# Up products of a second MoE: a bilinear algorithm of 20 products in place of Strassen's 7, its output blocks gathered from five accumulating chains

## Chip, cores, metric

One core of one Trainium2 chip. The metric is the device time of one launch in microseconds (us), less is better. The engines are TensorE (PE: matmuls; PEld: its weight loads), VectorE (DVE), ScalarE (ACT), GpSimd (POOL) and SyncE (SP, which issues the DMAs).

## The reference, cut to what matters

A clustered attention and a first MoE make x of 1536 tokens by 512 features. The change lies in what follows, the second MoE, and in how its operands are prepared:

```python
def _moe2_ref(x, w_gate, w1, w2):        # x 1536x512, 8 experts, w1[e] 512x1024, w2[e] 1024x512
    logits = x @ w_gate
    logits = logits - logits.max()
    P = np.exp(logits)
    for _ in range(8):                   # Sinkhorn: the gate
        P /= P.sum(1, keepdims=True) + 1e-09
        P /= P.sum(0, keepdims=True) + 1e-09
        P *= N / E
    out = np.zeros((N, D), dtype=np.float32)
    for e in range(E):
        h = np.maximum(x @ w1[e], 0.0)   # the "up" products
        ye = h @ w2[e]                   # the "down" products
        out += P[:, e:e + 1] * ye
    return out
```

## The kernel before

Every fp32 operand of a matmul is held as two fp32r parts, a high one (rounded by ScalarE) and a low one (what is left, by a subtraction on GpSimd or VectorE). A product of two operands is three matmuls into one PSUM bank, high by low, low by high, high by high: `three`, lines 826 to 830, so nearly all matmuls of the profile stand at L828, L829 and L830.

x (the first MoE's output, `x2[0..3]`, one tile for each 128 features, tokens along the free dimension) stays in SBUF. The second MoE runs through 32 units, `seq`: 8 experts by 4 pairs of 128 hidden features. A unit n takes 512 features by 256 hidden features of w1 and 256 by 512 of w2, each brought by one DMA of 512 KB (`fetch_w`, line 963, on the SyncE queue, two buffers in all). `up_weights` (line 970) and `down_weights` (line 991) make the high parts on ScalarE and the low parts on GpSimd one unit ahead. `w_tile` hands out weight tiles from a ring of 10.

Up products. The tokens are cut in halves (rows 1 and 2 of a 2x2 block matrix, 768 tokens each) and the features in halves (columns). Units 1 to 31 use Strassen's algorithm in Winograd's form, `up_products` (line 1180): 7 products of block sums, with the sums of x (`s1` to `s4`) made once by `sum_blocks` (line 1043: additions on VectorE, splits on ScalarE and GpSimd), half of them while the first MoE ends and half in unit 0; the sums of the weights (`t1` to `t4`) are made for every unit. Each half of 768 tokens is done in two passes, 512 columns and then 256:

```python
    HALF = N // 2
    PASSES = [(0, TM), (TM, HALF - TM)]
    WAYS = {(0, 0): "uuuu", (0, 1): "uudddudddudd", 0: "uuduuduudud", 1: "uuddudududududd"}
```

Unit 0 runs without the algorithm (`up_blocks`, line 1171), as the sums aren't ready. A product sums over two blocks of 128 features, so it is 2 x 3 matmuls, 7 x 2 x 3 a pass. The results combine on VectorE (L1188 to L1205), `relu` (line 1166) makes the high part of h on ScalarE and the low part on VectorE (L1169). PSUM has four banks for the up products (`bank`, line 835, used in turn) and four for the down products (`pools["l2"]`).

Down products. `down` (line 1209): one step ("d") is one block of 128 tokens, 6 matmuls of 512 columns, and one VectorE operation that adds the result times the gate's weight to the accumulator (L1236; L1231 while the expert is the first). The steps of a pass are done during the next pass. `WAYS` (line 1246) writes out the order of up (u) and down (d) steps on TensorE by hand; the loop of lines 1247 to 1280 follows it and puts the weights' preparation, the DMAs and the gate's pieces between them. Nothing of the second MoE goes through the planner that orders the attention.

The gate. `gates` (line 1103) adds the last logits, transposes them and runs the eight Sinkhorn iterations, one piece at each `next(gate)` in units 0 to 3: a small matmul (L1141) and eight small VectorE operations (L1133 to L1148). Its PSUM tiles come from `bank`.

Of the kernel before, what the change touches and what calls it, by code (L numbers as in the profile page):

```python
# [151 lines left out]
def moe_kernel(ctx: ExitStack, tc: tile.TileContext, qk, nat, cen, wt, w123, wout, wgate, w1, w2, out):  # L152
# [681 lines left out]

    def bank(shape, name):

        l1_pools.append(l1_pools.pop(0))
        return l1_pools[0].tile(shape, F32, tag="l1", name=name)
# [118 lines left out]
    HALF = N // 2  # L957
    PASSES = [(0, TM), (TM, HALF - TM)]
# [10 lines left out]

    def up_weights(n):  # L970

        if n >= len(seq):
            return
        raw = raws.pop((0, n))
        src = {"b11": raw[:, 0, : 2 * P], "b21": raw[:, 0, 2 * P :], "b12": raw[:, 1, : 2 * P], "b22": raw[:, 1, 2 * P :]}
        use = ("b11", "b21", "b12", "b22")
        if n > 0:
            use = ("b11", "t2", "b21", "t3", "t1", "t4", "b22")
            ts = m_p.tile([P, 2 * MC], I32, tag="ta", name=f"ts{n}").bitcast(F32)
            ts = ts.rearrange("p (t d) -> p t d", t=4)  # L980
            src.update((f"t{k + 1}", ts[:, k]) for k in range(4))
            for t, a, b in (("t1", "b12", "b11"), ("t2", "b22", "t1"), ("t3", "b22", "b12"), ("t4", "t2", "b21")):
                nc.gpsimd.tensor_sub(src[t], src[a], src[b])
            yield
        for key in use:
            w = wop[n, key] = w_tile(f"wop{n}_{key}").rearrange("p (l d) -> p l d", l=2)
            nc.scalar.copy(w[:, 0], src[key])  # L987
            nc.gpsimd.tensor_sub(w[:, 1], src[key], f32(w[:, 0]))  # L988
            yield
# [28 lines left out]
    s_p = [ctx.enter_context(tc.tile_pool(name="s_p0", bufs=1, reuse_waits="tile"))]  # L1018
# [7 lines left out]
    def tmp(name, n):  # L1026
        return tmp_p.tile([P, TM], F32, tag="tmp", bufs=6, name=name)[:, :n]


    half = lambda d, h, o, n: [x2[d][:, l, h * HALF + o : h * HALF + o + n] for l in range(2)]  # L1030
    sums = {}

    def operand(key, k, o, n):

        if key in ("a11", "a12", "a21", "a22"):
            return half(2 * (int(key[2]) - 1) + k, int(key[1]) - 1, o, n)
        if key == "s1":
            return half(k, 1, o, n)
        return [sums[key, k][:, l, o : o + n] for l in range(2)]

    s1_tile = {}

    def sum_blocks(k, i, late):

        o, n = PASSES[i]
        if i == 0:
            for key in ("s2", "s3", "s4"):
                sums[key, k] = s_p[k].tile([P, 2, HALF], F32R, tag=key, name=f"{key}_{k}")
            if late is not None:
                s1_tile[k] = tmp_p.tile([P, HALF], F32, tag="s1", name=f"s1_{k}")  # L1050
        v = {}

        def made(key, fn, *args):
            v[key] = tmp(f"{key}_{o}_{k}", n) if late is None or key != "s1" else s1_tile[k][:, o : o + n]
            fn(v[key], *args)

        def split(key):
            hi, lo = operand(key, k, o, n)
            nc.scalar.copy(hi, v[key])
            nc.gpsimd.tensor_sub(lo, v[key], f32(hi))  # L1060

        for key in ("a21", "a22", "a11", "a12"):
            made(key, nc.vector.tensor_add, *map(f32, operand(key, k, o, n)))
            yield
        made("s1", nc.vector.tensor_add, v["a21"], v["a22"])
        yield
        made("s3", nc.vector.tensor_sub, v["a11"], v["a21"])
        yield
        made("s2", nc.vector.tensor_sub, v["s1"], v["a11"])
        yield  # L1070
        made("s4", nc.vector.tensor_sub, v["a12"], v["s2"])
        yield
        for key in ("s2", "s3", "s4"):
            split(key)
            yield
        if late is None:
            split("s1")
        else:
            late.append(lambda: split("s1"))

    kept = []
    first = up_weights(0)
    blocks = iter(())
    for n, _ in enumerate(mixed):
        if n == M_LAST - drain + 1:
            blocks = iter(g for i in range(2) for g in sum_blocks(0, i, kept))
        for _ in range(2):
            next(blocks, None)
        if n >= M_LAST - drain + 2 and n % 4 == 0:
            next(first, None)  # L1090
    for _ in (*first, *blocks):
        pass
# [4 lines left out]
    s_p.append(ctx.enter_context(tc.tile_pool(name="s_p1", bufs=1, reuse_waits="tile")))  # L1097
# [3 lines left out]


    def gates():
# [6 lines left out]
        tt = bank([P, NT, 2, E], "tt")  # L1110
# [9 lines left out]
        tp = bank([P, P], "gtp")  # L1120
# [4 lines left out]
        bc = bank([P, 1], "gbc")  # L1125
# [5 lines left out]
        for it in range(SINKHORN):  # L1131
# [7 lines left out]
            cs = bank([P, NT, E], f"cs{it}")  # L1139
# [12 lines left out]
    def product(ps, n, key, xkey, o, c, first):  # L1152
        for k in range(2):
            w = wop[n, key][:, :, k * P : (k + 1) * P]
            hi, lo = operand(xkey, k, o, c)
            three(ps, w[:, 0], w[:, 1], hi, lo, first and k == 0, k == 1, not first)

    hs = {}

    def h_tile(n, i, key, c):  # L1160

        h = h_p.tile([P, c // (2 * P), 2, 2 * P], F32R, tag=f"h{i}", bufs=4, name=f"h{n}_{i}_{key}")
        hs[n, i, key] = h
        return h

    def relu(h, z):
        z = z.rearrange("p (s t) -> p s t", t=2 * P)
        nc.scalar.activation(h[:, :, 0], z, AF.Relu)  # L1168
        nc.vector.scalar_tensor_tensor(h[:, :, 1], z, 0.0, f32(h[:, :, 0]), op0=ALU.max, op1=ALU.subtract)  # L1169

    def up_blocks(n, i):
        o, c = PASSES[i]
        for key in ("21", "22", "11", "12"):
            ps = bank([P, TM], f"z{n}_{i}_{key}")[:, :c]
            product(ps, n, f"b1{key[1]}", f"a{key[0]}1", o, c, True)
            product(ps, n, f"b2{key[1]}", f"a{key[0]}2", o, c, False)
            relu(h_tile(n, i, key, c), ps)
            yield

    def up_products(n, i):  # L1180
        o, c = PASSES[i]
        x, y, z, w = (bank([P, TM], f"{t}{n}_{i}")[:, :c] for t in "xyzw")
        a, u2, u3, c22, c21, c12 = (tmp(f"{t}{n}_{i}", c) for t in ("a", "u2_", "u3_", "c22_", "c21_", "c12_"))
        product(x, n, "b11", "a11", o, c, True)
        nc.scalar.copy(a, x)
        yield
        product(y, n, "t2", "s2", o, c, True)
        nc.vector.tensor_add(u2, y, a)  # L1188
        yield
        product(x, n, "b21", "a12", o, c, False)  # L1190
        relu(h_tile(n, i, "11", c), x)
        yield
        product(y, n, "t3", "s3", o, c, False)
        nc.vector.tensor_add(u3, y, a)
        yield
        product(z, n, "t1", "s1", o, c, True)
        nc.vector.tensor_add(c22, z, u3)  # L1197
        relu(h_tile(n, i, "22", c), c22)
        yield
        product(w, n, "t4", "a22", o, c, True)  # L1200
        nc.vector.tensor_sub(c21, u3, w)
        relu(h_tile(n, i, "21", c), c21)
        yield
        product(z, n, "b22", "s4", o, c, False)
        nc.vector.tensor_add(c12, z, u2)  # L1205
        relu(h_tile(n, i, "12", c), c12)
        yield

    def down(n, i):
        e, p = seq[n]  # L1210
        o, c = PASSES[i]
        for r in (1, 0):
            for t in range(c // P):
                ts = slice(t % 2 * P, (t % 2 + 1) * P)
                tt = (r * HALF + o) // P + t
                last = n == len(seq) - 1

                pieces = 2 if last and i == 1 and r == 0 and t == c // P - 1 else 1
                for piece in range(pieces):
                    cs = slice(piece * DM // pieces, (piece + 1) * DM // pieces)  # L1220
                    l2 = pools["l2"].tile([P, DM], F32, tag="l2", name=f"l2_{n}_{r}_{o}_{t}_{piece}")[:, cs]
                    for j in range(2):
                        h, w = hs[n, i, f"{r + 1}{j + 1}"], wdn[n, j]
                        h = h[:, t // 2, :, ts]
                        three(l2, h[:, 0], h[:, 1], w[:, 0, cs], w[:, 1, cs], j == 0, j == 1)
                    a = acc[tt][:, cs]
                    if n == 0:
                        nc.scalar.copy(a, l2)
                    elif e == 0:

                        nc.vector.tensor_add(a, l2, a)  # L1231
                        if p == PAIRS - 1:
                            assert next(gate, None) is None
                            nc.vector.tensor_scalar(a, a, prob[:, tt, :1], None, op0=ALU.mult)
# [95 lines left out]
```

## Time and profile before

| | |
|---|---|
| three runs | 1450.41, 1451.54, 1452.12 us (median 1451.54) |
| profiled execution, span from first to last instruction | 1448.8 us |
| the second MoE in it, first up matmul to the end | 446.1 to 1448.8 us |
| busy in the span | TensorE 99%, VectorE 63%, GpSimd 42%, ScalarE 35% |

The span is the profiled execution's own time as its page gives it; a run's time is that and what lies before the first and behind the last instruction. A matmul's duration in a row overlaps that of the next one, as matmuls are pipelined: the distance between two starts is what one costs. In the same way two VectorE operations that follow each other without a wait start closer together than the first one's duration.

### The profile page before, as it was taken

The page shows a single profiled execution, that of the slowest core. Times are in us where ns is not written, and L with a number is a line of the kernel's source. Part 1 is how long each engine was busy: PE and PEld are TensorE (multiplying, and loading weights), DVE is VectorE, ACT ScalarE, POOL GpSimd, SP SyncE. Part 2 cuts the span into 40 slices and gives each one's busy share as a digit, 9 for nine tenths or more (in the row PEclk, how much of TensorE's full clock was granted, in tenths as well). Part 3 has the DMA queues.
Part 4 walks back from the last instruction along what each step waited for, and adds up shares of the span by engine and source line. Part 5 has one row for each costly group of instructions (what it writes and reads, how often), then busy time and mean ns, then how long its engine had stood idle before and what let it go on. Part 6 is the DMA issues. An engine that isn't in the chain of part 4 may idle for free.

```text
span 1448.8 us, 20593 instructions
## 1 busy us (share of the span) xinstructions
PE 1430.4 (99%) x7900; PEld 1199.8 (83%) x7900; DVE 912.0 (63%) x1627; ACT 510.8 (35%) x1115; POOL 602.2 (42%) x691
## 2 busy tenths in 40 slices
PE   6999999999999999999999999999999999999999
PEld 5778787888878888888888888888888888888887
DVE  6888885355448577665655565655565655665655
ACT  6778776122124422222222222222222222222221
POOL 7666641565637433233333233333233343333320
PEclk9999999999999999999999999999999999999999
DMA  8665621112120110000110000110000110000102
GB/s 247 175 162 153 161 57 40 47 58 74 51 67 30 44 45 30 29 30 29 45 44 30 30 29 30 44 44 30 29 30 30 45 44 30 30 30 30 44 15 87
DMA packets 32210, 83.26 MB, mean 57 GB/s; under 512 B 4688, under 2 KB 10224, under 8 KB 32112
## 3 DMA queue, kind: packets, MB, share of 16 engines
q1 hardware_dynamic: 32112, 81.95, 19.0%
q8 instruction: 62, 1.02, 0.3%
q14 instruction: 36, 0.29, 0.1%
HBM read 65.46 MB, written 3.19 MB: 47 GB/s over the span
## 4 chain that ended last, share of the span: by engine, by line
PE 96%; DMA 1%; POOL 1%; DVE 1%; ACT 0%; issue 0%; SPq 0%; POOLq 0%; DVEq 0%
PE l L828 12%; PE l L829 12%; PE l L830 12%; PE y L605 4%; PE t L591 4%; PE z L830 3%; PE z L829 3%; PE z L828 3%; PE m L828 3%; PE m L830 3%; PE m L829 3%; PE y L830 3%; PE x L830 3%; PE y L829 3%; PE x L829 3%; PE y L828 3%
## 5 line engine op out<-in xcount | busy, mean ns | idle before, releaser
L1236 DVE SCALAR_TENSOR_TENSOR acc<-l,prob,acc 128x512 f32<-128x512 f32 (+1 forms) x337 | 251.7, 747 | 126.1 <-PE l L830 122.7
L828 PE MATMUL l<-w,h 128*128 128x512 f32 (+1 forms) x770 | 302.5, 393 | 0.0
L829 PE MATMUL l<-w,h 128*128 128x512 f32 (+1 forms) x770 | 301.5, 392 | 0.0
L830 PE MATMUL l<-w,h 128*128 128x512 f32 (+1 forms) x770 | 299.2, 389 | 0.0
L1168 ACT ACTIVATE h<-c 128x512 fp32r<-128x512 f32 (+1 forms) x186 | 97.6, 525 | 368.6 <-DVE c L1197 190.7
L988 POOL TENSOR_TENSOR wop_t<-ts,wop_t 128x256 fp32r<-128x256 f32 x124 | 91.3, 746 | 244.2 <-ACT wop_t L987 244.2
L988 POOL TENSOR_TENSOR wop_b<-wraw,wop_b 128x256 fp32r<-128x256 f32 x97 | 79.3, 818 | 258.5 <-ACT wop_b L987 258.5
L1169 DVE SCALAR_TENSOR_TENSOR h<-c,h 128x512 fp32r<-128x512 f32 (+1 forms) x186 | 112.6, 605 | 110.0 <-ACT h L1168 110.0
L830 PEld LDWEIGHTS l<-w,h 128*128 128x128 f32 x770 | 144.6, 188 | 31.5
L828 PEld LDWEIGHTS l<-w,h 128*128 128x128 f32 x770 | 145.4, 189 | 24.4
L829 PEld LDWEIGHTS l<-w,h 128*128 128x128 f32 x770 | 145.4, 189 | 22.6
L998 POOL TENSOR_TENSOR w<-wraw,w 128x512 fp32r<-128x512 f32 x64 | 82.9, 1296 | 96.7 <-ACT w L997 96.7
L569 DVE TENSOR_SCALAR_CACHE_REDUCE e<-s 128x768 f32<-128x768 f32 x96 | 90.9, 951 | 19.2 <-PE s L558 12.0
L1168 ACT ACTIVATE h<-x 128x512 fp32r<-128x512 f32 (+1 forms) x62 | 30.4, 491 | 186.7 <-PE x L830 186.7
L577 ACT ACTIVATE e<-e,nm 128x768 f32<-128x768 f32 x96 | 89.7, 935 | 4.3 <-DVE e L569 4.0
L828 PE MATMUL m<-x,mhi 128*128 128x512 f32 x216 | 84.7, 392 | 0.4 <-POOL x L260 0.4
L591 PE MATMUL t<-ident,e 128*128 128x128 f32 x576 | 81.1, 277 | 3.4 <-ACT at L253 3.0
L830 PE MATMUL m<-x,mhi 128*128 128x512 f32 x216 | 84.1, 389 | 0.0
L829 PE MATMUL m<-x,mlo 128*128 128x512 f32 x216 | 84.1, 389 | 0.0
L830 PE MATMUL x<-x,wop_b 128*128 128x512 f32 (+1 forms) x248 | 83.3, 336 | 0.0
L830 PE MATMUL y<-s,wop_t 128*128 128x512 f32 (+1 forms) x248 | 83.3, 336 | 0.0
L829 PE MATMUL y<-s,wop_t 128*128 128x512 f32 (+1 forms) x248 | 83.3, 336 | 0.0
(201 smaller groups left out, 3025.9 us busy)
## 6 DMA issues: line engine op xcount, KB each, us to landing
wraw<-in_w SPq DMA_DIRECT2D x64, 512.0 KB, 4.0
mraw<-in_w SPq DMA_DIRECT2D x18, 512.0 KB, 3.6
raw<-in_qk SPq DMA_DIRECT2D x16, 384.0 KB, 4.0
nat<-in_nat SPq DMA_DIRECT2D x15, 384.0 KB, 4.3
v<-in_nat SPq DMA_DIRECT2D x16, 192.0 KB, 3.0
r<-row SPq DMA_DIRECT2D x16, 192.0 KB, 3.3
mraw<-in_wout SPq DMA_DIRECT2D x8, 384.0 KB, 3.0
opsb<-opm SPq DMA_DIRECT2D x15, 192.0 KB, 2.6
```

The costliest lines, as they stand in the source:

```text
L569: lambda e: nc.vector.tensor_scalar(ex(), scores(), -SCALE, None, op0=ALU.mult, op1=ALU.min, accum_out=nm()),
L577: lambda e: nc.scalar.activation(ex(), ex(), AF.Exp, bias=nm(), scale=-1.0, accum_out=sm()[:, n]),
L591: nc.tensor.transpose(t()[:, c, ks], ex()[:, c, ks], ident)
L605: nc.tensor.matmul(y()[c * D : (c + 1) * D], v()[:, c * (NQ // 2) + k], at()[:, :, c, k * P : (k + 1) * P], start=k == 0, stop=k == NQ // ...
L828: nc.tensor.matmul(ps, whi, xlo, start=first, stop=False, skip_group_check=more)
L829: nc.tensor.matmul(ps, wlo, xhi, start=False, stop=False, skip_group_check=more)
L830: nc.tensor.matmul(ps, whi, xhi, start=False, stop=last, skip_group_check=more)
L988: nc.gpsimd.tensor_sub(w[:, 1], src[key], f32(w[:, 0]))
L998: nc.gpsimd.tensor_sub(w[:, 1], raw[:, j], f32(w[:, 0]))
L1168: nc.scalar.activation(h[:, :, 0], z, AF.Relu)
L1169: nc.vector.scalar_tensor_tensor(h[:, :, 1], z, 0.0, f32(h[:, :, 0]), op0=ALU.max, op1=ALU.subtract)
L1236: nc.vector.scalar_tensor_tensor(a, l2, prob[:, tt, e : e + 1], a, op0=ALU.mult, op1=ALU.add)
```

## The change

The tokens are cut into three blocks of 512 (t = 0, 1, 2), the features into four of 128 (k), the hidden features of a unit into two of 128 (j). A 3x4 by 4x2 block product has 24 products of 128 by 128 by 512; the new algorithm has 20, each of one combination of x blocks (some are x's own blocks) and one combination of weight blocks. There is one pass of 512 columns, and each product is one `three`. The products are grouped in five chains; a chain is one PSUM bank into which its products add up, and what a bank holds after some of them is read by VectorE or ScalarE into the six output blocks, in SBUF, with a sign. Chain m has ten products, nine of them followed by a read on VectorE and one (10) by a read on ScalarE. Chains a, b, c and d share two banks, chain m takes two in turn, and the gate moves to the down products' banks. Unit 0 does the 24 products without the algorithm (`direct`).

```diff
+    SUMS = ("c20", "tmp", "c00", "c11", "c21", "c01", "c10")
+    cell = lambda t, k: [x2[k][:, l, t * TM : (t + 1) * TM] for l in range(2)]
...
+    CHAINS = {"a": (0, 17, 14), "b": (6, 3), "c": (12, 18), "d": (13, 5, 4), "m": (11, 19, 2, 10, 9, 7, 8, 1, 16, 15)}
...
+    def product(n, key):
+        c, i = CHAIN[key]
+        if i == 0:
+            sums[c] = chain("m" if c == "m" else "l1", [P, TM], f"{c}{n}")
+        ps = sums[c]
+        three(ps, *wop[n, key], *operand(key), i == 0, True, i > 0)
+        if key == 0:
+            nc.scalar.mul(take(n, "c01"), ps, -1.0)
+        elif key == 3:
+            vsub(take(n, "c21"), ps, cs["c01"])
+        elif key == 14:
+            nc.scalar.copy(take(n, "c11"), ps)
+        elif key == 18:
+            nc.scalar.copy(take(n, "c10"), ps)
+        elif key == 10:
+            nc.scalar.mul(take(n, "c20"), ps, -1.0)
+        elif key == 13:
+            nc.scalar.mul(take(n, "c00"), ps, -1.0)
+        elif key in MOVES_OF:
+            out, op, done = MOVES_OF[key]
+            op(cs[out], cs[out], ps)
+            if c == "m":
+                low()
+            if done:
+                relu(n, int(out[1]), int(out[2]), cs[out])
+
+    MOVES_OF = {
+        11: ("c01", vadd, False),
+        19: ("c11", vsub, False),
+        2: ("c21", vsub, False),
+        9: ("c10", vadd, True),
+        7: ("c11", vadd, True),
+        4: ("c20", vadd, False),
+        8: ("c21", vadd, True),
+        1: ("c20", vadd, True),
+        16: ("c00", vsub, True),
+        15: ("c01", vsub, True),
+    }
```

`relu` still makes the high part of h on ScalarE at once, but its low part on VectorE is put in a list, from which `low()` takes the oldest one later: with the next product of chain m that is read on VectorE, or with a down step. The unit's order is one list, in which a number is a product and d a down step; the first eight d belong to the unit before, the last four to this one:

```diff
-    WAYS = {(0, 0): "uuuu", (0, 1): "uudddudddudd", 0: "uuduuduudud", 1: "uuddudududududd"}
...
+    ORDER = "0 d 6 3 11 d 17 14 19 d 12 2 d 18 10 d 13 9 d 5 7 d 4 8 d 1 d 16 d 15 d d"
+    for n in range(1, len(seq)):
+        ups, up, down_w = 0, up_weights(n + 1), down_weights(n)
+        here = down(n)
+        for step in ORDER.split():
+            if step == "d":
+                ups += 1
+                next(later if ups <= 2 * TPB else here)
+                if ups in (1, 2 * TPB + 3):
+                    low()
+                continue
+            key = int(step)
+            product(n, key)
+            if key in (0, 17):
+                next(down_w)
+            if key in (19, 18, 4, 1, 16, 15):
+                next(up, None)
+            if key == 10:
                 fetch_w(1, n + 1)
...
+            if key == 16:
+                fetch_w(0, n + 2)
+            if n < PAIRS and key in (17, 12, 18, 13):
+                next(gate, None)
```

The weights of a unit come in six pieces, one at each `next(up, None)`; each combines blocks on GpSimd where it must, rounds on ScalarE and takes the low part on GpSimd. Two of the six:

```diff
+        t = scratch(2)
+        add(square(t), raw[:, :, 0::2], raw[:, :, 1::2])
+        split(t, *four((4, 5, 6, 3)))
+        yield
...
+        hi, lo = four((8, 2, 16, 9))
+        for part, src in enumerate((raw[:, 1, 0::3], raw[:, 0, 1:3])):
+            cs = slice(part * 2 * P, (part + 1) * 2 * P)
+            split(src, blocks(hi[:, cs]), blocks(lo[:, cs]))
```

The pieces are, in order, the weights of products 0 and 11 (two differences of 256 columns, of which one half is kept for the last piece); 18, 12, 17, 14 (a sum of 512); 4, 5, 6, 3 (a sum of 512); 1, 7, 19, 10 (a sum of 512); 8, 2, 16, 9 (plain blocks); 13 and 15 (the kept half).

The combinations of x are made once: `early()` while the first MoE ends (15 VectorE operations of 512 columns, 6 splits), `late()` in unit 0 (13 operations, 6 splits, four of them written over blocks of x that are no longer read). In unit 0 four down steps lie between the 24 products, the first of them behind `direct(1, 0)`, `direct(1, 1)` and `direct(2, 0)`.

## Rows read from the trace of the kernel before

**Rows 1.** The page: the span, and TensorE's busy time in it.
```profile
span 1448.8 us, 20593 instructions
...
PE 1430.4 (99%) x7900; PEld 1199.8 (83%) x7900; DVE 912.0 (63%) x1627; ACT 510.8 (35%) x1115; POOL 602.2 (42%) x691
```

**Rows 2.** Stretches: length, then busy time and instructions of each engine, clock, DMA share, GB/s.
```profile
446.10:480.40 34.30, 34.30 (x183) 28.43 (x182) 22.26 (x30) 19.91 (x46) 28.99 (x30) 1.00 0.18 56
...
912.99:943.99 31.00, 31.00 (x157) 26.42 (x156) 18.64 (x30) 8.41 (x19) 10.84 (x14) 1.00 0.11 35
...
480.40:1409.00 928.60, 928.60 (x4682) 791.16 (x4681) 574.65 (x971) 253.16 (x573) 324.87 (x390) 1.00 0.11 34
```

**Rows 3.** Timeline of TensorE, 901 to 914 us: start, duration, engine, line, operation.
```profile
901.13 0.28 PE L828 MATMUL x<-x,wop_b 128*128 128x256 f32 x1
...
901.49 0.28 PE L828 MATMUL x<-x,wop_b 128*128 128x256 f32 x1
...
912.99 0.39 PE L828 MATMUL x<-x,wop_b 128*128 128x512 f32 x1
...
913.67 0.39 PE L828 MATMUL x<-x,wop_b 128*128 128x512 f32 x1
```

**Rows 4.** Groups by form, 600 to 1440 us: count, then busy us, mean ns, idle before.
```profile
L988 POOL TENSOR_TENSOR wop_t<-ts,wop_t 128x256 fp32r<-128x256 f32 x104 | 75.9, 740 | 214.6 <-ACT wop_t L987 214.6
...
L998 POOL TENSOR_TENSOR w<-wraw,w 128x512 fp32r<-128x512 f32 x53 | 68.7, 1296 | 82.7 <-ACT w L997 82.7
...
L1169 DVE SCALAR_TENSOR_TENSOR h<-c,h 128x512 fp32r<-128x512 f32 x81 | 56.1, 692 | 56.6 <-ACT h L1168 56.6
...
L987 ACT CAST wop_t<-ts 128x256 fp32r<-128x256 f32 x104 | 41.6, 403 | 0.0
```

**Rows 5.** Timeline of TensorE and VectorE, 922 to 928 us.
```profile
922.29 0.39 PE L830 MATMUL z<-x,wop_t 128*128 128x512 f32 x1
...
922.71 0.69 DVE L1197 TENSOR_TENSOR c<-z,u 128x512 f32<-128x512 f32 x1 [0.61 <-PE z L830]
924.10 0.69 DVE L1169 SCALAR_TENSOR_TENSOR h<-c,h 128x512 fp32r<-128x512 f32 x1 [0.70 <-ACT h L1168]
924.71 0.68 DVE L1201 TENSOR_TENSOR c<-u,w 128x512 f32<-128x512 f32 x1
...
926.70 0.75 DVE L1236 SCALAR_TENSOR_TENSOR acc<-l,prob,acc 128x512 f32<-128x512 f32 x1
927.36 0.68 DVE L1205 TENSOR_TENSOR c<-z,u 128x512 f32<-128x512 f32 x1
```

**Rows 6.** Timeline of the attention's last transposes: ScalarE frees a bank, TensorE waits for it.
```profile
239.61 0.80 ACT L253 COPY at<-t 128x768 f32<-128x768 f32 x1 [0.43 <-PE t L591]
...
240.47 0.88 PE L591 MATMUL t<-ident,e 128*128 128x128 f32 x6 [0.89 <-ACT at L253]
```

**Rows 7.** Timeline of GpSimd and VectorE, 456 to 460 us, where both work on SBUF.
```profile
456.69 1.19 POOL L988 TENSOR_TENSOR wop_b<-wraw,wop_b 128x256 fp32r<-128x256 f32 x1
...
457.20 1.22 DVE L1055 TENSOR_TENSOR s<-s,a 128x512 f32<-128x512 f32 x1
...
457.84 1.74 POOL L1060 TENSOR_TENSOR x<-s,x 128x512 fp32r<-128x512 f32 x1
...
458.46 1.67 DVE L1055 TENSOR_TENSOR s<-a,s 128x512 f32<-128x512 f32 x1
```

**Rows 8.** Line 1169: count, duration ns min/median/max, first and last start us.
```profile
L1169 DVE SCALAR_TENSOR_TENSOR h<-c,h x186: 424/692/875, 488.1 to 1438.4; 128x512 fp32r<-128x512 f32 x93, 128x256 fp32r<-128x256 f32 x93
```

**Rows 9.** Timeline of VectorE, two of the gate's eight iterations.
```profile
500.39 0.24 DVE L1143 TENSOR_REDUCE c<-cs 128x8 f32<-128x96 f32 x1
...
502.33 0.68 DVE L1231 TENSOR_TENSOR acc<-l,acc 128x512 f32<-128x512 f32 x1
...
506.01 0.25 DVE L1143 TENSOR_REDUCE c<-cs 128x8 f32<-128x96 f32 x1
...
509.76 0.68 DVE L1231 TENSOR_TENSOR acc<-l,acc 128x512 f32<-128x512 f32 x1
```

More of the change, by code (lines that the diff above doesn't have):

```diff
@@ L991, in down_weights @@
+        yield
+        split(diff[:, : 2 * P], *pair((13, 15)))
     def down_weights(n):
@@ L1041, in moe_kernel @@
[L1041 to L1077, printed above, removed]
-        else:
-            late.append(lambda: split("s1"))
@@ L1083, in moe_kernel @@
+    combos = c_p
+    start = first_weights()
     blocks = iter(())
@@ L1085, in moe_kernel @@
         if n == M_LAST - drain + 1:
-            blocks = iter(g for i in range(2) for g in sum_blocks(0, i, kept))
-        for _ in range(2):
-            next(blocks, None)
+            blocks = early()
+        next(blocks, None)
         if n >= M_LAST - drain + 2 and n % 4 == 0:
-            next(first, None)
-    for _ in (*first, *blocks):
+            next(start, None)
+    for _ in (*start, *blocks):
         pass
@@ L1150, in gates @@
             )
[L1152 to L1207, printed above, removed]
@@ L1209, in down, with relu @@
-    def down(n, i):
-        e, p = seq[n]
[L1211 to L1218, printed above, removed]
+    hs, cs = {}, {}
+    lows = []
+    def relu(n, t, j, z):
+        h = hs[n, t, j] = h_p.tile([P, 2, TM], F32R, tag=f"h{t}{j}", name=f"h{n}_{t}{j}")
+        nc.scalar.activation(h[:, 0], z, AF.Relu)
+        lows.append(
+            lambda: nc.vector.scalar_tensor_tensor(h[:, 1], z, 0.0, f32(h[:, 0]), op0=ALU.max, op1=ALU.subtract)
+        )
@@ new lines, in low, with direct @@
+    def low():
+        if lows:
+            lows.pop(0)()
+    def direct(t, j):
+        ps = bank([P, TM], f"z{t}{j}")
+        x = [cell(t, k) for k in range(ND)]
+        for k in range(ND):
+            three(ps, *wop[0, k, j], *x[k], k == 0, k == ND - 1)
+        relu(0, t, j, ps)
+    CHAINS = {"a": (0, 17, 14), "b": (6, 3), "c": (12, 18), "d": (13, 5, 4), "m": (11, 19, 2, 10, 9, 7, 8, 1, 16, 15)}
+    CHAIN = {key: (c, i) for c, keys in CHAINS.items() for i, key in enumerate(keys)}
+    sums = {}
@@ new lines, in moe_kernel, with down @@
+    MOVES_OF = {
[10 more added lines that the diff above has]
+    }
+    def down(n):
+        e, p = seq[n]
+        last = n == len(seq) - 1
+        for block in (1, 2, 0):
+            for t in range(TPB):
+                tt = block * TPB + t
+                ts = slice(t * P, (t + 1) * P)
+                pieces = 2 if last and block == 0 and t == TPB - 1 else 1
@@ new lines, in moe_kernel, with more @@
+    blocks = late()
+    def more(n):
+        for _ in range(n):
+            next(blocks, None)
+    fetch_w(1, 1)
+    for _ in down_weights(0):
+        pass
+    up = up_weights(1)
+    direct(1, 0)
+    next(gate)
+    more(3)
+    low()
+    direct(1, 1)
+    next(gate)
+    more(3)
+    low()
+    next(up)
+    direct(2, 0)
+    more(3)
+    low()
+    next(up)
+    later = down(0)
+    next(later)
+    next(later)
+    direct(2, 1)
+    more(4)
+    low()
+    next(up)
+    next(later)
@@ L1281, in moe_kernel @@
+    while lows:
+        low()
     for _ in later:
```

226 lines of the change are left out of this document (147 added, 79 removed).

## Prediction

> **What bounds the kernel now.** First the page: TensorE is busy for 1430.4 of 1448.8 us [rows 1]. Then the stretches: in the second MoE the busy time equals the length, at a granted clock of 1.00; one unit of work (a pair of feature blocks of one expert, 31 of them behind the first) takes 31.00 us, and 30 units measured together 928.60 us, 30.95 each [rows 2]. VectorE is busy for 18.64 us of that unit, ScalarE for 8.41, GpSimd for 10.84 [rows 2]. So the end is set by how many matmuls there are and at what pitch they start; the other engines matter only if they make TensorE wait. The timeline gives the pitch: three 512-column matmuls start in 0.68 us (0.227 each), three 256-column ones in 0.36 (0.12 each) [rows 3]. Half the columns cost 53%, not 50%.
>
> **What the change removes.** A unit has 84 up matmuls now (7 products x 2 x 3, once at 512 and once at 256 columns) and 72 down matmuls of 512. By the pitches: 42 x 0.227 + 42 x 0.12 + 72 x 0.227 = 30.9 us, and the row says 31.00; the rest is a slightly wider pitch of down matmuls among narrow ones. After it there are 20 x 3 = 60 up matmuls, all of 512 columns, and the same 72: 132 x 0.2267 = 29.92 us. Saved: 1.08 us by the measured unit, 0.96 by the pitches alone. I take the row: 31 x 1.08 = 33.5 us (30 at the lower end). Unit 0 has no algorithm either way: 48 of 512 and 48 of 256 become 72 of 512, 16.6 to 16.3, another 0.3 us. Together 33.8 us. The Trainium skill (TensorE: Matmul & The Clock Gate, "Back-to-back issue gap") puts the warm gap of one matmul at columns / 2.4 GHz + 2.5 ns, which for these counts would be an estimate of 0.69 us a unit and 21 us in all; the rows here show a wider gap at both widths, and so more gained by having fewer matmuls.
>
> **What it adds beside TensorE.** VectorE: per unit 11 chain reads, 6 low halves of h and 12 accumulations. Back to back, a read or a low half takes 0.61 us and an accumulation 0.66 [rows 5]: 18.3 us against 18.64 now. GpSimd: 3 sums of 512 columns, 2 differences of 256, low halves of 3 x 512 and 4 x 256 columns and 2 x 512 for the down weights, at 1.30 and 0.74 us [rows 4]: 14.9 us against 10.84. ScalarE: 9216 columns against 6656, 8.41 x 9216 / 6656 = 11.6 us. All lie below 29.9 and cost nothing as totals. The two weight fetches are issued at products 10 and 16 of the unit, and their first readers come at product 0 and product 19 of the next, over 10 us later, on a queue that holds little else: nothing. The weights of a unit fill the ring of 10 tiles exactly, so each is rewritten just after its last product; the tightest is products 1, 7, 19, 10, rewritten after product 1 and read again by product 19 some 14 us later: nothing.
>
> **What it adds in TensorE's way.** Chain m stays in one bank over ten products, and VectorE reads it between them. The next product on it can't start before that read has ended, and as TensorE works in order, every matmul behind it stands too, the down matmuls included. From the start of a product: its last matmul starts 0.45 us later, the read 0.42 after that [rows 5], takes 0.69, and the bank's release reaches TensorE in about 0.06 (a ScalarE copy ends at 240.41, the transposes start at 240.47) [rows 6]. So 1.62 us must pass. The order gives 2.72 us or more between readers on m up to product 8 (a down step of 6 matmuls, 1.36, and two products), but only 2.04 on the last three links, 8 to 1, 1 to 16, 16 to 15 (one down step, one product). Slack there: 0.4 us. On such a link VectorE has a read, a low half and an accumulation, 0.61 + 0.61 + 0.66 = 1.88 of 2.04 us. It fits if nothing stretches them.
>
> GpSimd may. Where both worked from SBUF, an addition of VectorE took 1.22 and one 1.67 us instead of 0.69, and the GpSimd operation between them 1.74 instead of 1.30 [rows 7, 4]. Each ended about one operation after the other engine's did. The low halves are such operations (two SBUF inputs); reads and accumulations take one input from PSUM and have their plain length in all of [rows 5]. In the steady units of now, the 512-column low half still has a mean of 692 ns and the line's longest is 875 [rows 4, 8], but GpSimd is idle two thirds of the time there, and half in the new one. The new weights fall on the tight links: after products 4, 1, 16 and 15 come about 6 us of GpSimd work in 10 us. I place it: the low half after 8 becomes ready 0.6 us before GpSimd is done with the weights made after 4, so the read of product 1 is 0.45 late against 0.4 of slack, which makes 0.1 us; the low half after product 1 meets no GpSimd operation, the one after 16 waits 0.7 us, and product 15 ends the chain, whose next one is in the other bank. Taken: 0.1 us x 31 = 3 us. Bounds: 0, and 0.3 x 31 = 9 for a few tenths of misplacement.
>
> **Gate.** Eight iterations, now some 4 to 6 us apart, come up to four a unit behind products 17, 12, 18 and 13, with 2.7 us of products between the last three. An iteration takes VectorE 1.94 us (500.39 to 502.33) and, with GpSimd in the way, 3.75 (506.01 to 509.76) [rows 9]; a read and an accumulation, 1.3 us, lie in the same gap. Undisturbed they fit to 0.3 us, stretched they don't, by up to 2 us. Four iterations lie in such gaps: 0 to 8 us, and 2 taken, as GpSimd is busy behind product 18 alone.
>
> **Unit 0 and before.** The sums of x behind the first MoE and in unit 0 are some 28 VectorE operations of 512 columns and 12 low halves on GpSimd, where there were 32 and 16 (half of 512, half of 256). The down steps of unit 0 begin earlier, behind two products' low halves. GpSimd is busy for 28.99 of 34.30 us there already [rows 2], so VectorE's operations stretch as in rows 7. Bounds 0 to 4 us, 1.5 taken, about one such stretch in TensorE's way.
>
> **Sum.** 1448.8 - 33.8 + 3 + 2 + 1.5 = 1421.5 us of span; the runs' median, 1451.54, stands 2.7 us above the profiled span, which I keep: **1424 us**.
>
> **Rivals.** (a) The tight links wait more: GpSimd comes 0.3 to 0.4 us later or earlier than I place it and both links lose, some 0.5 us a unit, 15 us in all: 1418 + 15 + 3.5 = 1436. For it: 0.16 us of free time per link. Against: the mean of the low half now. (b) Slower than before: if on the links from 8 to 15 each low half waits out a whole 1.30 us operation, a link takes 0.61 + 1.30 + 0.61 + 0.66 = 3.18 instead of 2.04 us; the first loses 0.77 behind its slack, the second 1.14, 1.9 us a unit, 59 us in all: 1418 + 59 + 3.5 = 1480. It decides from 33.8 / 31 = 1.09 us a unit. Against it: GpSimd's work there is broken by waits for ScalarE, and VectorE's own operations hold it back as well (1.74 in rows 7). The Trainium skill (SBUF — State Buffer, "SBUF: two separate sides") states that rule: the port pair is locked for a whole instruction and the loser fully blocks. Rows 7 agree with it, rows 8 show a kernel placed so that it hardly bites. (c) The gate and unit 0 cost their upper ends and more, 14 us once: 1418 + 3 + 14 = 1435. That the change doesn't do what it says would show as more than 60 up matmuls a unit; the products counted in the diff leave no room for it.
>
> **Chances.** Forecast 0.78, (a) 0.13, (b) 0.04, (c) 0.05. The range: 1416, with no wait at all and 1.5 us of spread between runs, to 1435, with 9 us on the links, 8 on the gate and nothing more elsewhere; the upper halves of (a) and (c) and all of (b) stay outside, some 0.15. A measurement of this kernel tells 0.2%, 2.9 us, from no change. Faster by more: 0.94; within it 0.02, slower 0.04, both from (b).
>
> **What would show it.** Right: steady units of 29.9 to 30.1 us, three starts in 0.68 us throughout, and TensorE's only waits before products 16 and 15 (for line reads of chain m) and near the gate's iterations. Wrong: units above 30.3 us with waits for VectorE's reads on every link, low halves with a mean well above 0.8 us, or gaps of several us between 445 and 490 us.

## Result and the profile after

| | before | after |
|---|---|---|
| median of four runs each, side by side | 1451.44 us | 1432.11 us (1431.41 to 1432.90) |
| ratio | | 0.9867, 95% interval 0.9853 to 0.9881 |
| span of the profiled execution | 1448.8 us | 1430.5 us |
| first up matmul to the end, in that execution | 1002.7 us | 984.4 us |

The kernel became 1.3% faster, 19.3 us. That lies inside the range and 8.1 us above the predicted 1424. Of all the runs below one execution, the profiled one of the run with a single gate iteration, took 3540.10 us; it enters no figure here, and so that run has no usable trace. The page of the changed kernel, beside [rows 1]:

```profile
span 1430.5 us, 19248 instructions
...
PE 1402.4 (98%) x7132; PEld 1148.0 (80%) x7132; DVE 988.6 (69%) x1590; ACT 576.8 (40%) x1138; POOL 731.7 (51%) x716
```

TensorE's busy time fell by 28.0 us, the span by 18.3 only. TensorE now stands still for 9.7 us more, and busy time holds a stretch at half clock besides. The stretches say where (columns as in [rows 2]):

```profile
900.00:930.00 30.00, 30.00 (x134) 24.82 (x133) 20.93 (x30) 10.54 (x20) 15.05 (x15) 1.00 0.12 36
...
446.10:600.00 153.90, 144.42 (x633) 115.18 (x632) 117.22 (x199) 59.18 (x114) 85.40 (x75) 0.99 0.12 35
...
600.00:1425.00 825.00, 824.65 (x3635) 681.82 (x3634) 576.14 (x802) 285.26 (x540) 396.79 (x371) 1.00 0.12 37
```

From 600 us on TensorE is hardly ever out of work: 824.65 of 825.00. The idle time lies between 446 and 600, in units 0 to 4. The starts of product 6 in the timeline give the period of each unit, from one unit's product 6 to the next one's (the other columns are experiments, told below; their unit 1 of "both direct" has no product 6):

```
unit            after   no late sums   both direct   neither late sums nor gate
1               38.00      32.63            -              31.12
2               32.51      32.51          34.52            29.92
3               31.70      31.70          31.69            31.16
4               30.63      30.66          30.66            30.64
5 and later     29.95      29.95          29.95            29.94
```

27 units run at 29.95 us against 31.00 before: 28.4 us saved. 9.8 us of it are given back before unit 5: that unit begins at 607.3 us here, with eight down steps of unit 4 still to do, and at 603.0 before, with four, and four down steps take 5.4 us. TensorE's waits from 446 us to the end, without two of 0.3 us and less (waited for, total us, times, longest):

```profile
PE cs L1222 <- DVE prob L1219: 3.0, 2, 2.0
...
PE a L828 <- ACT c L1274: 2.0, 1, 2.0
PE b L828 <- DVE h L1241: 1.6, 1, 1.6
...
PE m L828 <- DVE c L1287: 1.3, 2, 1.0
PE l L829 <- DVE h L1241: 1.3, 1, 1.3
```

Seven waits. Reads of chain m (L1287) make TensorE wait twice, in units 3 and 4, and in no later one. L1222 is a gate iteration, L1241 a low half of h, L1274 ScalarE's read of product 0.

**The steady links.** The timeline of VectorE and GpSimd over the links 8 to 1, 1 to 16 and 16 to 15 of one unit, and the line of the low halves (count, ns min/median/max):

```profile
1018.57 1.08 DVE L1241 SCALAR_TENSOR_TENSOR h<-c,h 128x512 fp32r<-128x512 f32 x1
...
1020.23 0.67 DVE L1287 TENSOR_TENSOR c<-c,m 128x512 f32<-128x512 f32 x1
1020.83 0.68 DVE L1241 SCALAR_TENSOR_TENSOR h<-c,h 128x512 fp32r<-128x512 f32 x1
...
1022.69 1.31 DVE L1241 SCALAR_TENSOR_TENSOR h<-c,h 128x512 fp32r<-128x512 f32 x1
```
```profile
1017.81 1.29 POOL L1012 TENSOR_TENSOR wop<-ts,wop 128x512 fp32r<-128x512 f32 x1 [4.96 <-ACT wop L1011]
1019.06 1.75 POOL L1028 TENSOR_TENSOR ts<-wraw 128x512 f32<-128x512 f32 x1
1022.16 1.29 POOL L1012 TENSOR_TENSOR wop<-ts,wop 128x512 fp32r<-128x512 f32 x1 [1.35 <-ACT wop L1011]
```
```profile
L1241 DVE SCALAR_TENSOR_TENSOR h<-c,h x186: 675/686/1327, 501.7 to 1415.5; 128x512 fp32r<-128x512 f32 x186
```

The low half after 8 is stretched by 0.4 us, the one after 1 not at all, the one after 16 by 0.6: where the prediction put them (0.6, none, 0.7). Both stretched ones begin during a GpSimd operation and end 0.55 us behind it (1019.65 behind 1019.10, 1024.00 behind 1023.45). The read of product 1 (1020.23 to 1020.90) still ends in time for product 16 at 1021.17.

**The start.** The timeline of VectorE, GpSimd and ScalarE around product 6 of unit 1 (476.51), which needs the bank of unit 0's fifth block, with the two rows of TensorE that waited:

```profile
470.67 1.79 DVE L1155 TENSOR_TENSOR s<-s,s 128x512 f32<-128x512 f32 x1
471.87 1.74 POOL L1024 TENSOR_TENSOR ts<-wraw 128x512 f32<-128x512 f32 x1
472.49 1.67 DVE L1111 SCALAR_TENSOR_TENSOR s<-s,s 128x512 f32<-128x512 f32 x1
473.64 0.62 ACT L1011 CAST wop<-ts 128x512 fp32r<-128x512 f32 x1 [3.10 <-POOL ts L1024]
...
475.12 0.61 ACT L1239 ACTIVATE h<-z 128x512 fp32r<-128x512 f32 x1
...
475.76 0.69 DVE L1241 SCALAR_TENSOR_TENSOR h<-z,h 128x512 fp32r<-128x512 f32 x1 [1.61 <-ACT h L1239]
...
476.51 0.50 PE L828 MATMUL b<-x,wop 128*128 128x512 f32 x1 [1.60 <-DVE h L1241]
...
478.82 1.28 POOL L1028 TENSOR_TENSOR ts<-wraw 128x512 f32<-128x512 f32 x1
480.13 0.62 ACT L1011 CAST wop<-ts 128x512 fp32r<-128x512 f32 x1 [2.88 <-POOL ts L1028]
...
481.57 0.58 ACT L1274 ACTIVATE c<-a 128x512 f32<-128x512 f32 x1
...
482.21 0.50 PE L828 MATMUL a<-x,wop 128*128 128x512 f32 x1 [1.99 <-ACT c L1274]
```

Sums of x on VectorE (L1155, L1111) and a sum of weights on GpSimd (L1024) stretch each other to 1.7 to 1.8 us. ScalarE's cast of that weight sum (473.64) stands ahead of the relu (475.12), for which the low half waits (475.76), for which TensorE waits (476.51). The next weight sum (478.82) is late by then, and the read of product 0 (481.57) stands behind its cast. A third such wait is the gate's first iteration, with what followed, windows and timeline:

```profile
489.60:492.60 3.00, 0.94 (x5) 0.35 (x3) 2.33 (x6) 2.11 (x5) 2.27 (x3) 0.96 0.06 26
492.60:495.80 3.20, 3.15 (x8) 2.48 (x8) 2.96 (x8) 0.60 (x1) 2.05 (x2) 0.50 0.00 0
```
```profile
483.51 3.52 SPq L972 DMA_DIRECT2D wraw<-in_w  x2
...
487.51 0.73 POOL L1015 TENSOR_TENSOR ts<-wraw 128x256 f32<-128x256 f32 x1 [0.83 <-DMA wraw<-in_w]
...
488.97 0.41 ACT L1011 CAST wop<-ts 128x256 fp32r<-128x256 f32 x1 [4.32 <-POOL ts L1016]
...
489.76 0.38 ACT L1211 ACTIVATE prob<-lg,gnm 128x96 f32<-128x96 f32 x1
...
491.73 0.26 DVE L1219 TENSOR_TENSOR prob<-prob,rr 128x96 f32<-128x96 f32 x1
...
492.05 0.47 PE L1222 MATMUL cs<-prob,ones 128*128 128x96 f32 x2 [1.97 <-DVE prob L1219]
...
492.64 0.79 PE L828 MATMUL m<-x,wop 128*128 128x512 f32 x1
...
495.80 0.40 PE L829 MATMUL l<-w,h 128*128 128x512 f32 x1
```

The gate's exponential (489.76) stands behind a cast that had waited 4.32 us for GpSimd. GpSimd had waited for unit 2's weights (487.51): their fetch was issued at 483.51, when the last low half taken from unit 1's raw weights was done and the buffer free. TensorE was busy for 0.94 of 3.00 us; then its granted clock was 0.50, the 1.2 GHz level, up to 495.80. Seven matmul starts took 3.16 us there, 492.64 to 495.80, against 7 x 0.227 = 1.59 at full clock: 1.6 us more, beside the wait.

### The profile page after: what moved, and what is told of

It is laid out like the page before. It is cut to its first block, busy times and chain, and to the rows that moved or that the text cites. A ratio compares the mean times of both kernels' runs of the same rounds, so it can differ in the third digit from the quotient of the medians.

```text
span 1430.5 us, 19248 instructions
## 1 busy us (share of the span) xinstructions
PE 1402.4 (98%) x7132; PEld 1148.0 (80%) x7132; DVE 988.6 (69%) x1590; ACT 576.8 (40%) x1138; POOL 731.7 (51%) x716
## 4 chain that ended last, share of the span: by engine, by line
PE 91%; DVE 4%; POOL 2%; DMA 1%; ACT 1%; issue 1%; SPq 0%; POOLq 0%; DVEq 0%
PE l L828 12%; PE l L830 12%; PE l L829 12%; PE m L828 8%; PE m L830 8%; PE m L829 8%; PE y L605 5%; PE t L591 5%; PE s L555 2%; PE s L558 2%; PE d L828 1%; PE d L830 1%; PE d L829 1%; PE a L828 1%; PE a L830 1%; PE a L829 1%
## 5 line engine op out<-in xcount | busy, mean ns | idle before, releaser
L1012 POOL TENSOR_TENSOR wop<-ts,wop 128x512 fp32r<-128x512 f32 (+1 forms) x155 | 166.1, 1072 | 388.5 <-ACT wop L1011 388.5
L1287 DVE TENSOR_TENSOR c<-c,m 128x512 f32<-128x512 f32 x279 | 190.3, 682 | 95.9 <-PE m L830 92.4
L1239 ACT ACTIVATE h<-c 128x512 fp32r<-128x512 f32 x186 | 117.7, 633 | 235.6 <-DVE c L1287 235.6
L1241 DVE SCALAR_TENSOR_TENSOR h<-c,h 128x512 fp32r<-128x512 f32 x186 | 170.0, 914 | 0.0
L828 PE MATMUL m<-x,wop 128*128 128x512 f32 x310 | 122.3, 394 | 1.4 <-DVE c L1287 1.3
L830 PE MATMUL m<-x,wop 128*128 128x512 f32 x310 | 121.1, 391 | 0.0
L829 PE MATMUL m<-x,wop 128*128 128x512 f32 x310 | 121.0, 390 | 0.0
L569 DVE TENSOR_SCALAR_CACHE_REDUCE e<-s 128x768 f32<-128x768 f32 x96 | 90.9, 951 | 19.3 <-PE s L558 12.0
L1011 ACT CAST wop<-ts 128x512 fp32r<-128x512 f32 (+1 forms) x155 | 82.1, 529 | 32.2 <-PE d L829 14.9
```

The costliest lines, as they stand in the source:

```text
L569: lambda e: nc.vector.tensor_scalar(ex(), scores(), -SCALE, None, op0=ALU.mult, op1=ALU.min, accum_out=nm()),
L828: nc.tensor.matmul(ps, whi, xlo, start=first, stop=False, skip_group_check=more)
L829: nc.tensor.matmul(ps, wlo, xhi, start=False, stop=False, skip_group_check=more)
L830: nc.tensor.matmul(ps, whi, xhi, start=False, stop=last, skip_group_check=more)
L1012: nc.gpsimd.tensor_sub(lo, src, f32(hi))
L1239: nc.scalar.activation(h[:, 0], z, AF.Relu)
```

## Experiments

Three questions: do the steady links really stand at their limit, what part of the start's loss is the gate's, and what part is due to the sums of x in unit 0. Each kernel is timed against the kernel before, on the same chip.

**The gate.** Seven of its eight iterations are left out.

```diff
-SINKHORN = 8
+SINKHORN = 1
```

> The changed kernel with one gate iteration instead of eight; seven iterations (their small matmuls and VectorE operations) are left out of the computation. The changed kernel takes 1432.1 us, some 14 us more than its steady units promise, and all of that lies in units 0 to 4. Theory A (several causes, one after the other, the gate's own VectorE work the smaller one): seven pairs of gate matmuls (about 0.4 us each) and the wait of 1.2 us at 528 us go, perhaps the 1.1 us at 572 too; the waits at 474.5, 479.8 and 489.7 us stay: 1427 to 1428 us. Theory B (the gate's iterations, too close together, are the cause): 1422 us or less.

Measured: 1427.11 us (median of three), ratio 0.9834 (0.9818 to 0.9851). Seven iterations cost 5.0 us. Each has a pair of small matmuls, which sets the next starts back by 0.23 us in the timeline (0.69 us for the pair and two starts, against 2 x 0.227), so 1.6 us are their own matmuls, which the kernel before has as well. Some 3.4 are left for their waits and what follows from them. Theory B is out: the larger part of the loss lies elsewhere.

**The queues of unit 1.** The last weight pieces of unit 1 and the next fetch go behind product 0's read; the first two pieces for unit 2 come later.

```diff
-    for _ in up:
-        pass
-    fetch_w(0, 2)
+    rest = up
...
+            if n == 1 and key == 0:
+                for _ in rest:
+                    pass
+                fetch_w(0, 2)
-            if key in (19, 18, 4, 1, 16, 15):
+            if key in ((10, 13, 4, 1, 16, 15) if n == 1 else (19, 18, 4, 1, 16, 15)):
```

> In unit 1 alone: the last three pieces of its weights and the next fetch are put behind product 0's read on ScalarE instead of ahead of it, and the first two pieces of unit 2's weights behind products 10 and 13 instead of 19 and 18, so that ScalarE's in-order list doesn't stand behind GpSimd and a DMA. Theory A: the wait of 2.1 us at 479.8 (product 17 for ScalarE's read of chain a) and the one of 2.1 us at 489.7 (gate matmul for the exponential's followers), with the half clock of about 1.9 us behind it, go: 1426 to 1428 us. Theory B (the gate's chain on VectorE is late by itself): 1431 us or more, the wait at 489.7 stays.

Measured: 1429.18 us, ratio 0.9848 (0.9833 to 0.9862). The waits at 482.2 and 492.1 are gone, and the half clock with them, but a new one of 1.84 us stands before product 7 (497.05), where the read of product 9 (496.32) comes late behind two stretched operations of the gate (1.17 and 1.01 us). Some 3 us gained where 4 to 6 were expected.

**Low halves first.** In unit 0 each block's low half goes ahead of the sums of x, not behind them.

```diff
-    more(3)
     low()
+    more(3)
```

> In unit 0 the low half of h is put ahead of the sums of x in VectorE's list instead of behind them. Theory A: the waits of 1.4 us at 458.2 (down step for the low half) and 1.8 us at 474.5 (product 6 for a bank whose low half is late) go, and nothing else changes: 1429 to 1430 us. If instead the sums then come late and push the weights and the gate: 1432 us or more.

Measured: 1437.24 us, ratio 0.9903 (0.9888 to 0.9918): worse, as the second branch said. TensorE's wait at 459.9 went, and one of 5.9 us came before product 6. The timeline of VectorE, ScalarE and GpSimd shows the ring:

```profile
463.22 0.41 ACT L1011 CAST wop<-ts 128x256 fp32r<-128x256 f32 x1 [2.80 <-POOL ts L1016]
463.53 0.59 ACT L1239 ACTIVATE h<-z 128x512 fp32r<-128x512 f32 x1
...
464.15 0.69 DVE L1241 SCALAR_TENSOR_TENSOR h<-z,h 128x512 fp32r<-128x512 f32 x1 [4.39 <-ACT h L1239]
...
465.48 0.69 DVE L1149 TENSOR_TENSOR s<-s,s 128x512 f32<-128x512 f32 x1
466.26 0.62 ACT L1102 CAST x<-s 128x512 fp32r<-128x512 f32 x1 [2.14 <-DVE s L1149]
466.96 1.29 POOL L1103 TENSOR_TENSOR x<-s,x 128x512 fp32r<-128x512 f32 x1 [2.52 <-ACT x L1102]
468.20 1.29 POOL L1020 TENSOR_TENSOR ts<-wraw 128x512 f32<-128x512 f32 x1
469.53 0.62 ACT L1011 CAST wop<-ts 128x512 fp32r<-128x512 f32 x1 [2.65 <-POOL ts L1020]
```

The low half waits for ScalarE's relu, the relu stands behind a weight cast, the cast waits for GpSimd's sum, that sum stands behind a split of x, the split waits for ScalarE's cast of x, and that for VectorE's sum, which now stands behind the low half. No operation shown here is stretched (0.69, 1.29); the waits come from the order of the lists.

**The gate's places.** Its four iterations of a unit go behind products 11, 12, 9 and 8, further apart.

```diff
-            if n < PAIRS and key in (17, 12, 18, 13):
+            if n < PAIRS and key in (11, 12, 9, 8):
```

> The gate's pieces at evenly spread places of a unit (behind products 11, 12, 9 and 8, at least 5.4 us apart) instead of behind 17, 12, 18 and 13. Theory A: only the wait of 1.2 us at 528 and part of the one at 489.7 go: 1429 to 1431 us. Theory B (the close spacing is the main cause): 1424 us or less.

Measured: 1435.17 us, ratio 0.9886 (0.9869 to 0.9902), 3 us worse than the changed kernel; neither expectation held. Chain m pays, by the waits:

```profile
PE m L828 <- DVE c L1287: 7.4, 5, 2.6
```

Three of the four new places (11, 9, 8) lie behind products of chain m itself, so an iteration on VectorE comes just where the next read of that chain has to be in time; the change's own places (17, 12, 18, 13) lie behind products of other chains.

**Unit 0 rearranged.** Low halves first, GpSimd's sums of weights one place ahead of their casts, and the edit of the queues.

```diff
+        if n == 1:
+            yield
         split(t, *four((18, 12, 17, 14)))
```

> Unit 0 with its in-order lists untangled: low halves of h ahead of the sums of x on VectorE, each GpSimd sum for unit 1's weights issued one place earlier than its rounding on ScalarE, the last weights behind product 0, and unit 2's first pieces behind products 10 and 13. Theory C (in unit 0 ScalarE's rounding of h stands behind a weight rounding, that behind a GpSimd sum, that behind GpSimd's split of x, that behind a VectorE sum, and the low half, for which TensorE waits, behind all of it): the waits at 458.2, 474.5 and 479.8 us (1.4, 1.8, 2.1) go and most of the 4 us around 490: 1424 to 1427 us. If VectorE simply has too much to do in unit 0 whatever the order: 1430 us or more, with a wait of several us before unit 1's product 6.

Measured: 1432.70 us, ratio 0.9870 (0.9855 to 0.9885). The waits for the low half (1.3 us) and for product 0's read (2.0) went; product 6 now waits for its own weights:

```profile
PE b L829 <- POOL wop L1012: 1.9, 1, 1.9
PE b L828 <- ACT wop L1011: 1.6, 1, 1.6
```

So this order moves the wait and doesn't remove it. Two more mixtures end in the same way. With the gate at 0, 17, 2 and 13 on top of this:

> The kernel of the run on unit 0 and, in addition, the gate's pieces behind products 0, 17, 2 and 13 (4 us and more apart, none near the tight links) instead of 17, 12, 18 and 13. Theory A: the wait of 1.2 us in unit 2 goes and part of what is left in unit 1: 1 to 3 us less than the run on unit 0, 1422 to 1426 us. If the gate's place doesn't matter: the same as the run on unit 0.

it took 1432.43 us (ratio 0.9868, 0.9853 to 0.9882). And with the edit of the queues and only the first two low halves first:

> The run on ScalarE's list in unit 1 (1429.2 us) and, in addition, the first two low halves of unit 0 ahead of the sums of x. Only the wait of 1.4 us at 458.2 goes: 1428 us. Under theory D the sums then come later by as much and the wait turns up again before product 6: 1429 to 1430 us.

it took 1430.26 us (ratio 0.9858, 0.9844 to 0.9873): the wait of 1.3 us at 460 went, and that before product 6 grew from 1.6 to 3.2. That no order at all removes the loss is not shown by these runs.

**The links at their limit.** Product 15 follows 16 directly.

```diff
-    ORDER = "... 4 8 d 1 d 16 d 15 d d"
+    ORDER = "... 4 8 d 1 d 16 15 d d d"
```

> In every unit product 15 directly behind product 16 on chain m, the down step between them moved behind 15. By the prediction's loop (0.45 + 0.42 + 0.69 + 0.06 = 1.62 us from a product's start to the release of its bank) product 15 then waits 1.62 - 0.68 = 0.94 us or a little more in each of 31 units: 29 to 35 us more than the changed kernel's 1432.1, so 1461 to 1467 us. If the read of a bank doesn't hold TensorE as reckoned (a shorter loop, or one hidden): 1445 us or less.

Measured: 1467.83 us, ratio 1.0110 (1.0093 to 1.0127). A steady unit takes 31.03 us, 1.08 more than after, and the waits are where they should be:

```profile
PE m L828 <- DVE c L1287: 26.9, 32, 2.3
```

The loop of 1.62 us, worked out from [rows 5, 6], gave 0.94. One step of order costs more than the whole algorithm gains.

**GpSimd doubled.** The weight sum made on the tight links is done twice.

```diff
-        add(
+        for _ in range(2):
+            add(
```

> The GpSimd sum of 512 columns for the weights of products 1, 7, 19 and 10 is done twice (same result), so that a GpSimd operation of 1.3 us starts just when the low half after product 1 is ready, in every unit. Theory L (a low half waits out the whole GpSimd operation, and the tight links have about 0.4 us of slack): that low half takes 1.9 us or more, the read of product 16 comes 1.2 us late, product 15 waits 0.4 us (0.2 to 1.2) in each unit: 1444 us (1438 to 1469). If the two engines share without a whole wait, or the slack is larger: 1432 to 1434 us.

Measured: 1433.15 us, ratio 0.9873 (0.9858 to 0.9887); steady units 29.93 us, no wait on the links. The 1444 us of theory L did not come. The timeline of the two engines, and a window of the doubled line alone (GpSimd's busy time and instructions, clock, DMA share, GB/s):

```profile
1018.95 3.60 POOL L1029 TENSOR_TENSOR ts<-wraw 128x512 f32<-128x512 f32 x2
...
1020.71 0.68 DVE L1242 SCALAR_TENSOR_TENSOR h<-c,h 128x512 fp32r<-128x512 f32 x1
```
```profile
1020.69:1020.75 0.06, 0.00 (x0) 1.00 0.00 0
```

The pair's first operation, itself stretched by the low half after 8, ends at 1020.68 and the second begins at 1020.76. The low half after 1 starts at 1020.71, as soon as the read ahead of it lets it, and so in the gap between the two: it keeps its 0.68 us because no GpSimd operation is in progress, and the second sum is stretched in its place (1.78 us). The edit missed the low half that it aimed at, so theory L's rule, a wait for the whole operation, was not tested here. The longest low half takes 1.77 us, against 1.33 in the changed kernel.

**No late sums.** The sums of x of unit 0 are left out; six products read plain blocks of x instead. The matmuls stay the same in number and size.

```diff
-    blocks = late()
+    blocks = iter(())
+    for key, t, k in ((12, 0, 3), (19, 1, 1), (10, 1, 3), (2, 1, 2), (9, 2, 0), (16, 2, 2)):
+        xop[key] = t, k
```

> The second half of the sums of x (13 VectorE operations, 6 splits, all in unit 0) is left out; the six products that need them read plain blocks of x instead, so the result is another one, with the same matmuls. Theory D (unit 0 has too much for VectorE and GpSimd, whatever the order, and this is most of the 14 us): the waits at 458.2, 474.5, 479.8 and most of those around 490 go, 1422 to 1425 us. If the weights and ScalarE's list alone make them late: 1428 us or more.

Measured: 1424.53 us, ratio 0.9818 (0.9802 to 0.9835), 7.6 us below the changed kernel by the medians: the price of the late sums in this arrangement. That it meets the predicted 1424 is in part chance (the account below). Unit 1 takes 32.63 in place of 38.00 us (table above): more than half of the price is paid in unit 1, after the sums are done. No clock below 1.00 is left:

```profile
446.10:600.00 153.90, 150.31 (x668) 120.40 (x667) 109.86 (x198) 60.26 (x115) 79.69 (x73) 1.00 0.12 35
```

**Two units without the algorithm.** Unit 1 does 24 products like unit 0, and the late sums are spread over both. The edit also gives unit 1 plain weights, two splits in place of six pieces with sums, puts the low halves of h first and moves the gate's pieces. Its core:

```diff
-    for n in range(1, len(seq)):
+    for n in range(2, len(seq)):
```

> Unit 1 also without the algorithm, like unit 0: 12 matmuls more (2.7 us), but the second half of the sums of x is spread over units 0 and 1, and unit 1's weights need two splits instead of six pieces with sums. Theory D: some 9 us of waits in units 0 and 1 go for 2.7 us of matmuls and one unit's saving: 1424 to 1427 us. If the waits only move on to unit 2: 1432 us or more.

Measured: 1427.23 us (1425.81 to 1428.01), ratio 0.9837 (0.9822 to 0.9852), faster than before and than the changed kernel. The changed kernel's waits for the low halves of unit 0 and for product 0's read are gone. It stands 2.7 us above the kernel without late sums, and its 12 further matmuls are 12 x 0.227 = 2.7 us, so in the sum the late sums cost nothing more. As its unit 2 is 2.0 us longer (34.52 against 32.51) and the weights of unit 1 are lighter, which part of the edit helped is not shown.

**Neither late sums nor gate.** Both leavings-out together.

> Both suspects left out together: the late sums of x (as in the run without them, six products read plain blocks of x) and seven of the gate's eight iterations. Theory D (the steady part is as predicted, and late sums and gate are the whole of what units 0 to 4 lose, each for itself): 1432.1 less 7.6 less 4.7 = 1419.8, so 1419 to 1421, with units 1 to 4 at 30.0 to 30.5 us each. If the two compete for the same time of VectorE, so that either alone already takes away part of the other's waits: above that, 1421.5 to 1424, or, if each hid behind the other, below 1419. If something else in units 0 to 4 still loses (fetches, down weights, unit 1's sums of weights): unit 1 longer than 31 us with neither of them there.

Measured: 1419.56 us, ratio 0.9782 (0.9768 to 0.9795). The two costs add up: 1432.1 less 7.6 and 5.0 is 1419.5 (the expectation took 4.7 for the gate). So they are separate. Unit 1 is longer than the 30.5 us expected, and than the 31 of the last branch, but not for a wait: TensorE is busy throughout, with 139 matmul entries against 134, the gate's first small matmuls being in this unit.

```profile
474.18:505.30 31.12, 31.12 (x139) 25.30 (x138) 18.01 (x31) 16.58 (x33) 17.66 (x18) 1.00 0.17 51
505.30:535.22 29.92, 29.92 (x134) 24.78 (x133) 20.34 (x29) 10.47 (x21) 14.97 (x14) 1.00 0.12 35
```

Units 3 and 4 are above 30 us without any gate iteration in them, with the same two waits on chain m, 1.3 us, that the changed kernel has (above). In its timeline, ahead of the first of them, VectorE scales the finished first expert by the gate, SBUF to SBUF:

```profile
570.91 1.58 DVE L1328 TENSOR_SCALAR acc<-acc,prob 128x512 f32<-128x512 f32 x1
572.41 0.68 DVE L1287 TENSOR_TENSOR c<-c,m 128x512 f32<-128x512 f32 x1
```

One further operation on a link with 0.16 us to spare, and it takes 1.58 us there, 0.49 at 579.03; GpSimd had an operation from 570.92 on. That it is the cause was read from these rows; no run took it away.

## Why the prediction was right, and where it failed

By its own steps, in microseconds of the profiled execution:

| step | predicted | measured |
|---|---|---|
| saved by fewer matmuls, a steady unit | 1.08 | 1.05, with its waits |
| tight links, 31 units | 3 (0 to 9) | 1 |
| gate | 2 (0 to 8) | 3.4 |
| unit 0 | 1.5 (0 to 4) | 7.6 by medians, 8.7 by two traces |
| units 3 and 4 without gate (scaling of the first expert, by the rows) | not seen | 1.9 |

- **Removed matmuls: right.** 29.92 us a unit was worked out from the pitches, 29.95 came. One reading beside it was wrong and did no harm: the 928.60 us of [rows 2] aren't 30 units, as unit 1 began at 476.17 and not at 480.40. From unit 3 on every unit took 31.00, which is what the sum used.
- **Links: the model right, its size too high.** The difference of 0.03 us a unit makes 1 us at most, against 3. The low halves met GpSimd where they were placed, and the first lost 0.4 instead of 0.6 us, which its slack of 0.4 took up. One sign was badly chosen: "a mean well above 0.8 us" came (170.0 us / 186 = 0.91) and meant nothing, as only lateness beyond the slack counts.
- **Rival (a), 0.5 us a unit: refuted** by units of 29.95. **Rival (b), the whole GpSimd operation on every link, 1.9 us a unit: refuted** by the same units. Two of the three low halves lose what was left of a GpSimd operation, 0.4 and 0.6 us, and one meets none. The trace agrees with the rule of the Trainium skill (SBUF — State Buffer, "SBUF: two separate sides") that whichever comes second is held until the other's instruction is done: each of the 78 stretched low halves from 610 us on began during a GpSimd operation and ended 0.54 to 0.55 us behind it. Where these operations fell on the links decided the loss.
- **The failed step is "Unit 0 and before".** It compared the number of operations with before (28 against 32, 12 against 16) and allowed "about one such stretch in TensorE's way", 4 at most. Without the late sums the kernel takes 7.6 us less by the medians. From first up matmul to end it takes 984.4 us, without the late sums 975.7 (447.91 to 1423.6): 8.7, of which 1.6 are the half clock. These two traces differ by 1.8 us in where the first up matmul lies, with nothing changed ahead of it, so the price is 7.6 to 8.7. What the step left out: the lists of VectorE, ScalarE and GpSimd wait for each other in a ring, so one stretched sum delays weights, relu, low halves and the gate, and the delay is carried into unit 1, with the fetch of unit 2's weights, which "What it adds beside TensorE" put at nothing. The sums were costed as durations beside TensorE, while their time was set by the waits between three in-order lists. Why before had no such wait with as many sums was not tried. Totals don't tell: up to unit 1's first product GpSimd was busy for 27.51 of 30.07 us before (446.10 to 476.17; the 34.30 of [rows 2] reaches 4.2 us into unit 1) and for 20.28 of 26.71 here (446.06 to 472.77), VectorE for 21.39 and 21.93.
- **So the outcome is nearest to rival (c)**, "the gate and unit 0 cost their upper ends and more, 14 us once", to which 0.05 was given: 7.6 to 8.7 and 3.4 and 1.9, some 13 to 14 us once, though the gate stayed well below its upper end. The sign "gaps of several us between 445 and 490 us" came with it: 1.3, 1.6 and 2.0 us.
- **That the time lies in the range is in part luck.** Its upper end held 9 us on the links, 8 on the gate "and nothing more elsewhere". The links took 1 and the gate 3.4; what filled the range was unit 0, outside its own bounds of 0 to 4, and a cost that wasn't seen.
- **The account.** Predicted span 1421.5; 6.1 to 7.2 more in unit 0, 1.9 for units 3 and 4, 1.4 for the gate, 2 less on the links: 1428.9 to 1430.0. The span was 1430.5; 0.5 to 1.6 us stay unassigned. From span to median it was 1.6 us here, where 2.7 was kept.

## What to carry to other kernels

Check a new steady state link by link: time of the loop that frees a bank, against the distance in the written order; here that gave 29.95 us to 0.1. Then cost the start-up by itself, following every in-order list through each wait on the others. Taking one wait away mostly brought another: six other orders took 1429 to 1437 us, the best of them 2.9 us less than the changed kernel. One more plain unit, with the sums spread over two units and lighter weights, gained 4.9 at the price of 12 matmuls. For a long loop, even 9 us lost once are a third of a gain of 28.

## What the hardware showed unexpectedly

After three microseconds in which TensorE was busy for 0.94, its granted clock was 0.50 (1.2 GHz) for the next 3.2 us, so a 2 us wait cost 3.6. A wait of the same 2 us ahead of 482.21, with TensorE busy for 1.22 of 3.21 us (479.00 to 482.21), brought no fall: the granted clock was 1.00 up to 486.00. And a low half on VectorE that begins in the gap of 0.08 us between two GpSimd operations keeps its 0.68 us (1020.71), while the GpSimd operation behind it takes 1.78 us in place of 1.29: it matters which of the two begins first.
